# Two more products in two levels in group 4, and the last product in two levels from pieces loaded at the start of group 5

## The chip, the cores and the metric

The kernel runs on one core of one Trainium2 chip. A core has TensorE for matmuls, VectorE and ScalarE for elementwise work, GpSimd (POOL), and SyncE (SP); in this kernel the last two mostly issue DMAs, which sixteen DMA engines carry out. The metric is the device time of one execution in microseconds, as the median of several runs. Before the change it is 674.46 us (three runs, 673.37 to 674.55).

## What is computed

Linear attention with decay in blocks, and then an expert layer with the activation h - tanh(h):

```python
# q, k, v: (4, 8, 768, 64) float32; per head and block of 64 positions
intra = np.einsum('bhic,bhjc->bhij', qb, kb) * Dmask[None]
intra = np.einsum('bhij,bhjd->bhid', intra, vb)
inter = np.einsum('bhid,bhde->bhie', qb * lam_pow[None], kv_state)
out[:, :, sl] = intra + inter
kv_state = lam_block * kv_state + np.einsum('bhsd,bhse->bhde', kb_dec, vb)
...
x = attn_out.transpose(0, 2, 1, 3).reshape(3072, 512)
h = x @ w_in            # 512 x 2048
g = h - np.tanh(h)
return (g @ w_out)      # 2048 x 512
```

## The kernel before

**Groups.** The sequence of 768 is worked in six groups, g = 0 to 5, of 128 positions. With four batches a group holds 512 tokens. In each group the hidden layer has an "up" part (x times w_in, tanh) and a "down" part (times w_out). While group g is in its up and down parts, the attention of group g+1 is worked in pieces between them. Group 0 is computed plainly. In groups 1 to 5 the up and the down product are each done by a scheme of seven products instead of eight: the two factors are split into quarters, A11 to A22 and B11 to B22, sums S1 to S4 and T1 to T4 of quarters are formed, and P1 to P7 are multiplied: P1 = A11 B11, P2 = A12 B21, P3 = S4 B22, P4 = A22 T4, P5 = S1 T1, P6 = S2 T2, P7 = S3 T3.

**One level and two levels in the down part.** A product Pn of the down part is 256 tokens by 1024 hidden values by 256 outputs. `down` does it in one level: sixteen matmuls with 256 columns. `down_twice` uses the same scheme once more inside Pn: seven steps, 1 to 7, of four matmuls with 128 columns, in the order SUB = (1, 2, 6, 5, 7, 3, 4). For this it needs sums of quarters of the left factor (s1 to s4, by VectorE, 128 x 512 elements each) and of the right one. The latter are made once, in groups 1 to 4, by `factors_twice` (t1, t2, t3, t4), which writes them to the DRAM tensor `fine`; one-level factors lie in the DRAM tensor `factors`. `twice(g, n)` says which products are done in two levels. Before, P1 and P2 are so only in group 5, and P3 in every group but 1 and 5.

**Room for sums.** `sums_twice` (line 685) takes two tiles of a pool of four called "sums" and overwrites a quarter of the hidden layer for the third. P1 and P2 can't overwrite A11 and A12, which are used again; `sums_apart` (L699 to L702) takes four tiles for each, from the room of the q and k blocks, which is free in the last group. `factors_twice` (L593) takes three of the four "sums" tiles and makes t3 in the place of b12, a quarter that was loaded as a piece.

**Pieces.** The right factors come from DRAM in pieces of 256 KB by DMAs on GpSimd's queue, in a ring of seven places ("wb"). `pieces_of` gives the order of all pieces; `piece` issues loads up to seven ahead of their use. The quarters of the factor that `factors_twice` works on are pieces of this ring too. The fine factors of P1 are made in group 3, those of P2 in group 4, at fixed counts of the up products (`turns`).

**Banks.** A two-level product collects in two PSUM banks, y and zw. ScalarE copies y after steps 1, 6, 7 and 4 (L720), VectorE adds the parts of zw at the end (L727, L728). After P2, `first_out` adds P1 and P2 and stores a quarter of the output (L677), and `sums_once` (L636) forms S2 and later S4.

**Order in group 4 around the change.** In the up part, for each quarter u of the hidden layer, products 6, 5, 1 (of u+1), 7, 3 are worked; at u = 3 the down product P1 takes the place of product 1. Attention of group 5 comes in between: transposes of q and k by VectorE (L306), scores `sp` (L327), their mask (L331), outputs `op` (L375, L381). Then P2, P4, P5, P6, P7 and P3. Instructions are put in order by a list scheduler, for each engine, when the program is built[...].

**The end.** In group 5 `down_end` does P3 in one level, in three parts of 256, 128 and 128 columns; each is added to P5's result and stored on SP's queue while the next is multiplied.

The two conditions that the change edits:

```python
def twice(g, n):
    return n in TWICE and not (g == NG - 1 and n == 3) and not (g == 1 and n in (4, 7, 3)) and not (
        g < NG - 1 and n in (1, 2))
```

Of the kernel before, what the change touches and what calls it, by code (L numbers as in the profile page):

```python
# [16 lines left out]
BLK = 128  # L17
# [6 lines left out]
def kernel(  # L24
# [158 lines left out]
    SUB = (1, 2, 6, 5, 7, 3, 4)  # L183
    GI = 2
# [351 lines left out]
    def twice(g, n):  # L536
        return n in TWICE and not (g == NG - 1 and n == 3) and not (g == 1 and n in (4, 7, 3)) and not (
            g < NG - 1 and n in (1, 2))
# [8 lines left out]
    def pieces_of(g):  # L547
        if g >= GI:
            yield from ((g, ("in", 4), x) for x in (6, 5, 3))
        yield from ((g, ("quarter", t), x) for t in MADE_IN.get(g, ()) for x in range(4))  # L550
        for n in (1, 2, 4, 5, 6, 7):
            yield from ((g, n, x) for x in (SUB if twice(g, n) else range(NU)))
        if g == NG - 1:
            yield from ((g, 3, x) for x in range(NU))
            return
        for kind, x in in_turn(g):
            if kind == "down":
                yield g, 3, x
            elif x in (3, 5, 6):
                yield g + 1, ("in", 2), x  # L560
# [27 lines left out]
    def factors_twice(t):  # L588

        b11, b12, b21, b22 = (quarters.pop((t, i, j)) for i in range(2) for j in range(2))  # L590
        t1, t2, t4 = (late["pool"].tile([128, NU, 128], F32, name=f"wt{x}", tag="sums", bufs=4) for x in (1, 2, 4))
        for x, dst, a, b in ((5, t1, b12, b11), (6, t2, b22, t1), (7, b12, b22, b12), (4, t4, b21, t2)):
# [101 lines left out]
    def sums_apart(g, n):  # L694

        a11, a12, a21, a22 = quarter(g, n)
        s1, s2, s3, s4 = (late["blk"].tile([128, NP, BLK // 32, 32], F32, name="sblk", tag="blk").rearrange(
            "d p r a -> d p (r a)") for _ in range(4))
# [3 lines left out]
        nc.vector.tensor_tensor(s4, a12, s2, op=AL.subtract)  # L702
        low[g, n] = (s1, s2, s3, s4)

    def down_twice(g, n, zw):
        a11, a12, a21, a22 = quarter(g, n)
        apart = len(low[g, n]) == 4
        s1, s2, s3, s4 = low.pop((g, n)) if apart else (*low.pop((g, n)), a21, a12)
# [3 lines left out]
        for x, a, dst, keep in ((1, a11, y, o[:, 0:128]), (2, a12, zw[:, 0:128], None), (6, s2, y, o[:, 128:256]),  # L712
                                (5, s1, zw[:, 256:384], None), (7, s3, y, o[:, 384:512]), (3, s4, zw[:, 128:256], None),
                                (4, a22, y, o[:, 256:384])):
            wb = piece(g, n, x).rearrange("p m c -> p (m c)")
            for u in range(NU):
                nc.tensor.matmul(out=dst, lhsT=a[:, u, :], rhs=wb[:, ts(u, 128)], start=x in (1, 2) and u == 0,  # L717
                                 stop=u == NU - 1, skip_group_check=True)
            if keep is not None:
                nc.scalar.activation(keep, dst, AF.Copy)  # L720
            if x == 2 and not apart:
# [27 lines left out]

    def down_end(g):  # L750

        a, o = hidden(g, 21), res[g, 5].rearrange("q (m c) -> q m c", m=2)
        rows = out.rearrange("(b s) d -> s b d", b=B)[ts(g, BLK), 0:2, 256:512]
        wbs = [piece(g, 3, u) for u in range(NU)]
        for tag, m, c0, c1 in (("z", 0, 0, 256), ("w", 1, 0, 128), ("ya", 1, 128, 256)):
            t = bank("end", tag, 1)[:, 0:c1 - c0]
            for kt in range(KH):
                nc.tensor.matmul(out=t, lhsT=a[:, kt // 2, kt % 2, ts(m, 128)], rhs=wbs[kt // 2][:, kt % 2, c0:c1],
                                 start=kt == 0, stop=kt == KH - 1)
            nc.vector.tensor_tensor(o[:, m, c0:c1], o[:, m, c0:c1], t, op=AL.add)  # L760
            nc.sync.dma_start(out=rows[:, m, c0:c1], in_=o[:, m, c0:c1])
# [108 lines left out]
    for g in range(1, NG):  # L870
        last = g == NG - 1
        p0, p1 = attention(g + 1) if not last else ([], [])
# [93 lines left out]
```

## Time and profile before

| what | us | where it is read |
|---|---|---|
| median of three runs | 674.46 | times |
| profiled execution | 673.58 | times of the profiled run |
| its span, first to last instruction | 671.6 | page |
| TensorE, matmuls busy | 660.5 (98%) | page, part 1 |
| TensorE, weight loads busy | 576.3 (86%) | page, part 1 |
| VectorE busy | 491.2 (73%) | page, part 1 |
| ScalarE busy | 196.6 (29%) | page, part 1 |
| DMA, mean rate | 203 GB/s | page, part 2 |

The page shows one execution. Its span is shorter than the time measured, since some work lies before the first and after the last instruction. A matmul's recorded duration overlaps with the next one's, so the cost of a series is read from starts. "Idle before" in a timeline stands in brackets, with what ended it. The granted clock of TensorE is 1.000 over the whole run.

### The profile page before, as it was taken

How to read it: one execution, taken by the hardware profiler on the slowest of the kernel's cores; microseconds unless marked ns; L12 is line 12 of the kernel's file. 1: busy time of each engine (PE TensorE's matmuls, PEld its weight loads, DVE VectorE, ACT ScalarE, POOL GpSimd, SP SyncE). 2: the span in 40 equal slices, each digit the busy share in tenths (PEclk: the TensorE clock that was granted, in tenths of full speed). 3: DMA queues.
4: the chain of work that ended last, by engine and by line, in shares of the span. 5: the costliest groups of instructions: out<-in, count | busy, mean ns of one | idle time of the engine just before them, and what ended most of it. 6: DMA issues, size and time to landing. Idle time of an engine off the chain costs nothing.

```text
span 671.6 us, 13055 instructions
## 1 busy us (share of the span) xinstructions
PE 660.5 (98%) x4872; PEld 576.3 (86%) x4872; DVE 491.2 (73%) x892; ACT 196.6 (29%) x380; POOL 216.7 (32%) x373
## 2 busy tenths in 40 slices
PE   7899999999999999999999999999999999999998
PEld 6688855558888999987999988899988899988997
DVE  4798767993887772499896389988369978348963
ACT  4564433423331111333112242112333112334210
POOL 0001424217432424144345402254412244400451
PEclk9999999999999999999999999999999999999999
DMA  9979889869855977486998855597944686710695
GB/s 213 218 207 248 258 235 254 294 147 265 251 147 135 243 196 210 107 261 202 252 288 249 227 124 136 153 291 216 276 108 128 170 244 204 229 48 0 212 300 163
DMA packets 164958, 136.16 MB, mean 203 GB/s; under 512 B 134304, under 2 KB 135456, under 8 KB 164896
## 3 DMA queue, kind: packets, MB, share of 16 engines
q0 software_dynamic: 31216, 103.83, 48.8%
q1 hardware_dynamic: 133536, 31.50, 23.7%
q8 instruction: 39, 0.64, 0.4%
q14 instruction: 23, 0.19, 0.1%
q10 hardware_dynamic: 144, 0.00, 0.0%
HBM read 107.22 MB, written 28.05 MB: 201 GB/s over the span
## 4 chain that ended last, share of the span: by engine, by line
PE 81%; issue 9%; DMA 3%; POOL 3%; SPq 2%; DVE 1%; ACT 0%; POOLq 0%; DVEq 0%; ACTq 0%
PE y L433 11%; PE y L717 11%; PE op L795 8%; PE zw L717 8%; PE h L774 7%; PE z L433 7%; PE w L649 4%; PE y L649 4%; PE y L517 4%; PE plain L649 3%; PE sp L327 3%; PE op L381 3%; PE z L517 2%; POOL wb L614 2%; PE op L375 2%
## 5 line engine op out<-in xcount | busy, mean ns | idle before, releaser
L614 POOL DMA_DIRECT2D wb<-fine x161 | 86.7, 539 | 148.2 <-PE y L717 80.4
L441 ACT ACTIVATE th<-g 128x512 f32<-128x512 f32 x76 | 47.6, 630 | 94.8 <-DVE g L446 33.2
L433 PE MATMUL y<-xt,w 128*128 128x256 f32 x320 | 74.0, 380 | 0.0
L433 PEld LDWEIGHTS y<-xt,w 128*128 128x128 f32 x320 | 59.9, 190 | 9.0 <-ACT g L521 0.9
L720 ACT ACTIVATE q<-y 128x128 f32<-128x128 f32 x92 | 25.5, 277 | 133.8 <-PE y L717 132.9
L442 DVE TENSOR_TENSOR g<-g,th 128x512 f32<-128x512 f32 x76 | 51.8, 688 | 16.9 <-ACT th L441 16.8
L774 PE MATMUL h<-xt,w 128*128 128x256 f32 x256 | 56.5, 381 | 2.1 <-DVE w L271 2.1
L795 PE MATMUL op<-wt,g 128*128 128x512 f32 x128 | 56.5, 595 | 0.0
L774 PEld LDWEIGHTS h<-xt,w 128*128 128x128 f32 x256 | 48.2, 190 | 9.3 <-DVE w L271 1.5
L717 PE MATMUL y<-wb,g 128*128 128x128 f32 x416 | 55.4, 278 | 0.1
L717 PEld LDWEIGHTS y<-wb,g 128*128 128x128 f32 x416 | 50.5, 192 | 1.5 <-issue 0.6
L617 POOL DMA_DIRECT2D wb<-factors x48 | 25.9, 541 | 71.0 <-DVE wt L593 24.6
L795 PEld LDWEIGHTS op<-wt,g 128*128 128x128 f32 x128 | 23.8, 190 | 27.7 <-issue 26.5
L198 POOL DMA_DIRECT2D raw<-in_moe_w_out_dram x16 | 8.9, 553 | 91.0 <-DVE g L782 52.4
L433 PE MATMUL z<-tt,ws 128*128 128x256 f32 x160 | 38.1, 381 | 0.0
L433 PE MATMUL z<-xt,ws 128*128 128x256 f32 x160 | 37.9, 380 | 0.0
L433 PE MATMUL y<-tt,ws 128*128 128x256 f32 x160 | 37.8, 379 | 0.0
L717 PE MATMUL zw<-wb,g 128*128 128x128 f32 x272 | 35.9, 275 | 0.0
L331 DVE TENSOR_TENSOR ss<-sp,mask 128x512 f32<-128x512 f32 x48 | 31.0, 683 | 5.5 <-PE sp L327 5.5
L433 PEld LDWEIGHTS z<-xt,ws 128*128 128x128 f32 x160 | 30.2, 190 | 4.3 <-ACT g L449 0.2
L433 PEld LDWEIGHTS z<-tt,ws 128*128 128x128 f32 x160 | 29.6, 190 | 4.7 <-DVE g L469 0.8
L433 PEld LDWEIGHTS y<-tt,ws 128*128 128x128 f32 x160 | 30.1, 190 | 3.9
(181 smaller groups left out, 1325.6 us busy)
## 6 DMA issues: line engine op xcount, KB each, us to landing
wb<-fine POOLq DMA_DIRECT2D x161, 256.0 KB, 4.0
wb<-factors POOLq DMA_DIRECT2D x68, 256.0 KB, 4.6
raw<-in_moe_w_out_dram POOLq DMA_DIRECT2D x16, 512.0 KB, 5.1
v_nat<-in_v_dram SPq DMA_DIRECT2D x24, 256.0 KB, 5.3
factors<-wt POOLq DMA_DIRECT2D x8, 768.0 KB, 4.9
wb<-fine_in POOLq DMA_DIRECT2D x24, 256.0 KB, 4.2
fine<-wt POOLq DMA_DIRECT2D x21, 256.0 KB, 4.3
k_nat<-in_k_dram SPq DMA_DIRECT2D x20, 256.0 KB, 5.0
```

The source lines that it names most:

```text
L331: tied(g == 0, nc.vector.tensor_tensor(ss[:, j], sp[j], mask[:, j], op=AL.mult))
L433: nc.tensor.matmul(out=t[:, m, :], lhsT=wt[:, kt, ts(m, 128)], rhs=x[:, kt, :], start=first and m == 0 and kt == 0, stop=kt == 1, skip_gro ...
L441: nc.scalar.activation(th, src, AF.Tanh)
L442: nc.vector.tensor_tensor(dst(c), src, th, op=AL.subtract)
L517: nc.tensor.matmul(out=dst[:, ts(u, 128)], lhsT=a, rhs=b, start=x in (1, 2, 5) and u == 0, stop=True, skip_group_check=True)
L614: nc.gpsimd.dma_start(out=t.rearrange("p m c -> p (m c)"), in_=fine[TWICE.index(n_), SUB.index(x_)].rearrange("p u c -> p (u c)"))
L617: nc.gpsimd.dma_start(out=t, in_=factors[XAT[FACT[n_][1]]][:, 2 * x_:2 * x_ + 2, :])
L649: nc.tensor.matmul(out=t[:, m, :], lhsT=a[:, u, kt, ts(m, 128)], rhs=wb[:, kt, :], start=first and u == 0 and m == 0 and kt == 0, stop=u = ...
L717: nc.tensor.matmul(out=dst, lhsT=a[:, u, :], rhs=wb[:, ts(u, 128)], start=x in (1, 2) and u == 0, stop=u == NU - 1, skip_group_check=True)
L720: nc.scalar.activation(keep, dst, AF.Copy)
L774: tied(u == 0, nc.tensor.matmul(out=hm[c][:, m, :], lhsT=w1[u][:, i, a, ts(m, 128)], rhs=xt[0, t][:, i, :], start=m == 0 and i == 0, stop= ...
L795: nc.tensor.matmul(out=obank[b], lhsT=g, rhs=wt[:, 2 * a:2 * a + 2, :], start=kt == 0 and a == 0, stop=kt == KH - 1 and a == 1)
```

## The change

P1 and P2 are done in two levels in group 4 as well, and P3 in group 5. P1 and P2 work their steps in the order APART = (1, 5, 6, 2, 7, 3, 4). `sums_apart` makes three sums; the fourth is made inside the product after step 5, in the tile of s1. In group 4 the three tiles are those of k in natural layout, in group 5 blocks as before. `factors_twice` puts t3 in an own tile of the "sums" pool. `load_end`, called at the start of group 5, loads the seven fine pieces of P3 on SP's queue into the tiles of k and v; the four pieces of P3 leave GpSimd's stream. `down_end` does the seven steps from them, adds each quarter to P5's result as soon as it is complete, and stores it by itself.

```diff
--- before.py
+++ after.py
@@ -181,6 +181,8 @@
     factors = dram.tile([NX, 128, KH, 256], F32, name="factors")
 
     SUB = (1, 2, 6, 5, 7, 3, 4)
+
+    APART = (1, 5, 6, 2, 7, 3, 4)
     GI = 2
     TWICE = (3, 5, 6, 4, 7, 1, 2)
     fine = dram.tile([len(TWICE), len(SUB), 128, NU, 128], F32, name="fine")
@@ -534,8 +536,8 @@
     RING = 7
 
     def twice(g, n):
-        return n in TWICE and not (g == NG - 1 and n == 3) and not (g == 1 and n in (4, 7, 3)) and not (
-            g < NG - 1 and n in (1, 2))
+        return n in TWICE and not (g == 1 and n in (4, 7, 3)) and not (
+            g < NG - 2 and n in (1, 2))
 
     def in_turn(g):
 
@@ -549,9 +551,8 @@
             yield from ((g, ("in", 4), x) for x in (6, 5, 3))
         yield from ((g, ("quarter", t), x) for t in MADE_IN.get(g, ()) for x in range(4))
         for n in (1, 2, 4, 5, 6, 7):
-            yield from ((g, n, x) for x in (SUB if twice(g, n) else range(NU)))
+            yield from ((g, n, x) for x in (range(NU) if not twice(g, n) else APART if n < 3 else SUB))
         if g == NG - 1:
-            yield from ((g, 3, x) for x in range(NU))
             return
         for kind, x in in_turn(g):
             if kind == "down":
@@ -588,8 +589,9 @@
     def factors_twice(t):
 
         b11, b12, b21, b22 = (quarters.pop((t, i, j)) for i in range(2) for j in range(2))
-        t1, t2, t4 = (late["pool"].tile([128, NU, 128], F32, name=f"wt{x}", tag="sums", bufs=4) for x in (1, 2, 4))
-        for x, dst, a, b in ((5, t1, b12, b11), (6, t2, b22, t1), (7, b12, b22, b12), (4, t4, b21, t2)):
+        t1, t2, t3, t4 = (late["pool"].tile([128, NU, 128], F32, name=f"wt{x}", tag="sums", bufs=4)
+                          for x in (1, 2, 3, 4))
+        for x, dst, a, b in ((5, t1, b12, b11), (6, t2, b22, t1), (7, t3, b22, b12), (4, t4, b21, t2)):
             tc.keep_in_program_order(nc.vector.tensor_tensor(dst, a, b, op=AL.subtract))
             nc.gpsimd.dma_start(out=fine[TWICE.index(MADE[t]), SUB.index(x)], in_=dst)
             if MADE[t] in (1, 2) and x in (5, 6, 4):
@@ -693,31 +695,41 @@
 
     def sums_apart(g, n):
 
+
         a11, a12, a21, a22 = quarter(g, n)
-        s1, s2, s3, s4 = (late["blk"].tile([128, NP, BLK // 32, 32], F32, name="sblk", tag="blk").rearrange(
-            "d p r a -> d p (r a)") for _ in range(4))
+        if g == NG - 1:
+            sums = [late["blk"].tile([128, NP, BLK // 32, 32], F32, name="sblk", tag="blk").rearrange(
+                "d p r a -> d p (r a)") for _ in range(3)]
+        else:
+            sums = [io.tile([128, H, D], F32, name="sk", tag="k", bufs=3).rearrange("p (u v) d -> p u (v d)", u=NU)
+                    for _ in range(3)]
+        s1, s2, s3 = sums
         nc.vector.tensor_tensor(s1, a21, a22, op=AL.add)
         nc.vector.tensor_tensor(s2, s1, a11, op=AL.subtract)
         nc.vector.tensor_tensor(s3, a11, a21, op=AL.subtract)
-        nc.vector.tensor_tensor(s4, a12, s2, op=AL.subtract)
-        low[g, n] = (s1, s2, s3, s4)
+        low[g, n] = (s1, s2, s3)
 
     def down_twice(g, n, zw):
         a11, a12, a21, a22 = quarter(g, n)
-        apart = len(low[g, n]) == 4
-        s1, s2, s3, s4 = low.pop((g, n)) if apart else (*low.pop((g, n)), a21, a12)
+        apart = n < 3
+        s1, s2, s3, s4 = (*low[g, n], low[g, n][0]) if apart else (*low.pop((g, n)), a21, a12)
         y = bank("y2", "ya" if n in (4, 6, 3, 1) else "yb", 1)[:, 0:128]
         zw = bank("zw", zw, 1)
         o = res[g, n] = otile(f"q{n}")
-        for x, a, dst, keep in ((1, a11, y, o[:, 0:128]), (2, a12, zw[:, 0:128], None), (6, s2, y, o[:, 128:256]),
-                                (5, s1, zw[:, 256:384], None), (7, s3, y, o[:, 384:512]), (3, s4, zw[:, 128:256], None),
-                                (4, a22, y, o[:, 256:384])):
+        steps = {1: (a11, y, o[:, 0:128]), 2: (a12, zw[:, 0:128], None), 6: (s2, y, o[:, 128:256]),
+                 5: (s1, zw[:, 256:384], None), 7: (s3, y, o[:, 384:512]), 3: (s4, zw[:, 128:256], None),
+                 4: (a22, y, o[:, 256:384])}
+        order = APART if apart else SUB
+        for x in order:
+            a, dst, keep = steps[x]
             wb = piece(g, n, x).rearrange("p m c -> p (m c)")
             for u in range(NU):
-                nc.tensor.matmul(out=dst, lhsT=a[:, u, :], rhs=wb[:, ts(u, 128)], start=x in (1, 2) and u == 0,
-                                 stop=u == NU - 1, skip_group_check=True)
+                nc.tensor.matmul(out=dst, lhsT=a[:, u, :], rhs=wb[:, ts(u, 128)],
+                                 start=x in (1, 5 if apart else 2) and u == 0, stop=u == NU - 1, skip_group_check=True)
             if keep is not None:
                 nc.scalar.activation(keep, dst, AF.Copy)
+            if x == 5 and apart:
+                nc.vector.tensor_tensor(s4, a12, s2, op=AL.subtract)
             if x == 2 and not apart:
                 nc.vector.tensor_tensor(a12, a12, s2, op=AL.subtract)
             if x != STEPS[-1]:
@@ -747,18 +759,55 @@
         for _ in steps:
             pass
 
+    ends = {}
+
+    def load_end():
+
+        for x, tag, bufs in zip(SUB, "kkkvvvv", (3, 3, 3, 4, 4, 4, 4)):
+            t = ends[x] = io.tile([128, H, D], F32, name="wend", tag=tag, bufs=bufs).rearrange("p h d -> p (h d)")
+            nc.sync.dma_start(out=t, in_=fine[TWICE.index(3), SUB.index(x)].rearrange("p u c -> p (u c)"))
+
     def down_end(g):
 
-        a, o = hidden(g, 21), res[g, 5].rearrange("q (m c) -> q m c", m=2)
+        a11, a12, a21, a22 = quarter(g, 3)
+        s1, s2 = low.pop((g, 3))
+        y, zw = bank("y2", "ya", 1)[:, 0:128], bank("zw", "z", 1)
+        o, f = otile("q3"), res[g, 5]
         rows = out.rearrange("(b s) d -> s b d", b=B)[ts(g, BLK), 0:2, 256:512]
-        wbs = [piece(g, 3, u) for u in range(NU)]
-        for tag, m, c0, c1 in (("z", 0, 0, 256), ("w", 1, 0, 128), ("ya", 1, 128, 256)):
-            t = bank("end", tag, 1)[:, 0:c1 - c0]
-            for kt in range(KH):
-                nc.tensor.matmul(out=t, lhsT=a[:, kt // 2, kt % 2, ts(m, 128)], rhs=wbs[kt // 2][:, kt % 2, c0:c1],
-                                 start=kt == 0, stop=kt == KH - 1)
-            nc.vector.tensor_tensor(o[:, m, c0:c1], o[:, m, c0:c1], t, op=AL.add)
-            nc.sync.dma_start(out=rows[:, m, c0:c1], in_=o[:, m, c0:c1])
+
+        def add(c, src):
+            nc.vector.tensor_tensor(f[:, ts(c, 128)], f[:, ts(c, 128)], src, op=AL.add)
+
+        def leave(c):
+            nc.sync.dma_start(out=rows[:, c // 2, ts(c % 2, 128)], in_=f[:, ts(c, 128)])
+
+        for x, a, dst, keep in ((1, a11, y, 0), (2, a12, zw[:, 0:128], None), (6, s2, y, 1),
+                                (5, s1, zw[:, 256:384], None), (7, a21, y, 3), (3, a12, zw[:, 128:256], None),
+                                (4, a22, y, None)):
+            for u in range(NU):
+                nc.tensor.matmul(out=dst, lhsT=a[:, u, :], rhs=ends[x][:, ts(u, 128)], start=x in (1, 2) and u == 0,
+                                 stop=u == NU - 1, skip_group_check=True)
+            if keep is not None:
+                nc.scalar.activation(o[:, ts(keep, 128)], dst, AF.Copy)
+            if x == 2:
+                nc.vector.tensor_tensor(a12, a12, s2, op=AL.subtract)
+            elif x == 6:
+                add(0, o[:, 0:128])
+                add(0, zw[:, 0:128])
+                leave(0)
+            elif x == 5:
+                add(1, o[:, 128:256])
+                f5 = f.rearrange("q (i c) -> q i c", i=2)[:, :, 128:256]
+                nc.vector.tensor_tensor(f5, f5, zw[:, 256:384][:, None, :].to_broadcast([128, 2, 128]), op=AL.add)
+            elif x == 7:
+                add(3, o[:, 384:512])
+                leave(3)
+            elif x == 3:
+                add(1, dst)
+                leave(1)
+            elif x == 4:
+                add(2, dst)
+                leave(2)
 
 
     def up_plain(u, cs):
@@ -869,6 +918,8 @@
     up(1, 0, 1)
     for g in range(1, NG):
         last = g == NG - 1
+        if last:
+            load_end()
         p0, p1 = attention(g + 1) if not last else ([], [])
         for u in range(NU):
             if u + 1 == NU and twice(g, 1):
```

## The prediction

> **What bounds the kernel now.** I read the page's shares and chain first, then TensorE's timeline over the last two groups, then the timelines of the engines that feed it. Two lines of the page:
>
> ```profile
> PE 660.5 (98%) x4872; PEld 576.3 (86%) x4872; DVE 491.2 (73%) x892; ACT 196.6 (29%) x380; POOL 216.7 (32%) x373
> ...
> PE 81%; issue 9%; DMA 3%; POOL 3%; SPq 2%; DVE 1%; ACT 0%; POOLq 0%; DVEq 0%; ACTq 0%
> ```
>
> Matmuls hold 81% of the chain that ended last, and weight loads alone fill 86% of the span. The list of waits gives TensorE 7.7 us in the whole trace, all but 0.7 of it on tiles of the first stage (h, sp, idle, tp, kv). So TensorE's queue is the clock: what is taken out of it shortens the run, provided that nothing it needs comes late. TensorE's timeline, groups 4 and 5 (start, duration, engine, line, operation, tiles, shapes, count; a float32 matmul is two instructions, hence x32 for sixteen):
>
> ```profile
> 517.88 7.07 PE L649 MATMUL y<-wb,g 128*128 128x256 f32 x32
> 524.78 1.89 PE L433 MATMUL z<-xt,ws 128*128 128x256 f32 x8
> 526.60 2.06 PE L327 MATMUL sp<-qt,kt 64*128 64x128 f32 x32
> 528.59 7.17 PE L649 MATMUL w<-wb,g 128*128 128x256 f32 x32
> 535.69 1.10 PE L375 MATMUL op<-qd,state 64*64 64x128 f32 x32
> ...
> 554.47 1.06 PE L717 MATMUL zw<-wb,g 128*128 128x128 f32 x8
> 555.36 1.06 PE L717 MATMUL y<-wb,s 128*128 128x128 f32 x8
> ...
> 661.30 7.19 PE L758 MATMUL end<-wb,g 128*128 128x256 f32 x48
> ```
>
> Starts, not durations, give the cost: durations overlap. One-level P1 of group 4 takes 524.78 - 517.88 = 6.90, P2 535.69 - 528.59 = 7.10; a step of a two-level product takes 555.36 - 554.47 = 0.89, seven of them 6.25. Now VectorE in group 4:
>
> ```profile
> 512.93 0.69 DVE L442 TENSOR_TENSOR g<-g,th 128x512 f32<-128x512 f32 x1 [0.16 <-ACT th L441]
> ...
> 517.03 0.69 DVE L593 TENSOR_TENSOR wt<-wb,wt 128x512 f32<-128x512 f32 x1
> 517.63 0.70 DVE L306 STREAM_TRANSPOSE qt<-q_blk 128x512 f32<-128x512 f32 x1
> ...
> 521.21 0.68 DVE L451 TENSOR_TENSOR g<-g,y 128x512 f32<-128x512 f32 x1
> 521.81 0.68 DVE L452 TENSOR_TENSOR g<-g,y 128x512 f32<-128x512 f32 x1
> 522.41 0.68 DVE L636 TENSOR_TENSOR g<-gS,g 128x512 f32<-128x512 f32 x1
> 523.01 1.28 DVE L442 TENSOR_TENSOR g<-g,th 128x512 f32<-128x512 f32 x2
> ```
>
> Bracketed idle time is nearly absent: VectorE is 96% busy from 517.6 to 538.6 (20.09 of 21.0 us by the stretches' busy times), one operation per 0.60 us. This is the only place where the change meets a second full engine. Last, GpSimd's issues of pieces there:
>
> ```profile
> 486.75 1.73 POOL L617 DMA_DIRECT2D wb<-factors  x3
> 500.80 0.54 POOL L617 DMA_DIRECT2D wb<-factors  x1 [12.32 <-DVE wt L593]
> ...
> 509.74 0.54 POOL L617 DMA_DIRECT2D wb<-factors  x1 [2.11 <-DVE wb L593]
> 510.28 0.54 POOL L594 DMA_DIRECT2D fine<-wb  x1
> 514.39 0.54 POOL L617 DMA_DIRECT2D wb<-factors  x1 [3.58 <-DMA fine<-wb]
> 518.01 0.54 POOL L594 DMA_DIRECT2D fine<-wt  x1 [3.08 <-DVE wt L593]
> 518.55 0.54 POOL L617 DMA_DIRECT2D wb<-factors  x1
> ```
>
> The ring's seven places are shared with the four quarters from which P2's fine factors are made, so pieces come one by one as quarters are released.
>
> [...] so a wait put in VectorE's queue holds everything behind it, as at 175.02, where L593 waited 0.31 us for a store and L464 stood behind. [...] after SP's 256 KB store at 637.95 the landing of pieces rose from 2.9 to 5.2 us.
>
> **Part by part: TensorE.** P1: 6.90 to 6.25, -0.65. P2: 7.10 to 6.25 plus 0.10 for the switch of operand seen at such starts, -0.75. Last P3: 668.50 - 661.30 = 7.20 to 6.35, -0.85. Sum -2.25 us. The tail stays: a 128x128 add (0.29) and a 64 KB store (668.84 to 670.37) end both. The six other adds of the last product are 0.29 to 0.42 each and its a12 0.69; P7's four (2.2 us together) and these, 4.8 in all, fit in its 6.25 us, and its SP queue has six stores of 0.35 us. ScalarE's ten more copies of 0.28 us (3 for P1, 4 for P2, 3 for P3) hide under 29% load.
>
> **VectorE in group 4.** Added for each of P1 and P2: three sums and the fourth, 4 x 0.60, and two adds of the zw bank, about 0.38 each: 3.15, so 6.3 us together, where there is next to no idle time. What can give way is work that is due later: eight L636 (for P6 and P3) and P5's three sums, 6.6 us, all before 538.6. So it just fits, if the order is good. In group 5 the three sums of P1 stand between L452 and L469 at 615.80 to 619; the like place here is 512.7 to 516. They push the transposes by 1.8 - 0.3 = 1.5 us, to end at 522.7. Then L451, L452, s4 (ready after P1's step 5, which ends at 519.7) at 523.9 to 524.5, and the two L442, which complete A12, at 525.7. P1's step 3 wants s4 at 517.88 + 5 x 0.89 = 522.3; product 3 of up (1.73) and sp (1.99) are there to fill this. P2's first sum can run from 525.7 and its step 5 wants it at 517.88 + 6.25 + 1.73 + 1.99 + 0.89 = 528.7: 3.0 us for P4's two sums and P2's own. I take 0 for this, since group 5 ran P4's and P2's first sums right behind L442 (624.83 and 625.43); its bounds are 0 and 4.4 (below).
>
> **Pieces of P1.** Seven instead of four: three at 486.75, the fourth at 500.80, the fifth and sixth at about 509.7, since b12 is free after t3 and no longer at the landing of its store (514.39). The seventh waits for b21, read by t4 at 517.03, which the sums may push by 1.5: issue between 518.0 and 520.0, landing after 4.7 to 5.4 us (518.55 landed at 524.01), so 523 to 525.4 against a need at 523.25, or 525 with product 3 before it. Taken: +0.2; bounds 0 and 2.1. P2's pieces are issued from 519 on, at P1's steps, and are due from 528: covered.
>
> **t3's own tile.** It takes the fourth of four places called sums. In group 1 t3 would start at 174.02 but its place is freed by t1's store, which landed at 175.00; t4's by a store that landed at 177.41. If L464 stays behind t4, it goes from 175.63 to 178.0, and product 3, which adds to the bank that it reads, from 176.78 to 178.7: 1.9 us. If L464 goes ahead, nothing. The second set repeats this with 0.25. In group 2 twelve tiles instead of nine go through the four places (about 1.2 us at 295), but quarters come free earlier and may save its two TensorE waits, 0.54 and 0.15. Taken: +0.2 in all; bounds -0.7 and +3.3.
>
> **DMAs.** load_end puts 7 x 256 KB on SP's queue, idle from 529 to 638, where they start as soon as places come free: three at P2's end, two after att_out at 538, two at 563; all before the stretch 588 to 617 with 26 GB/s. In 538.6 to 551.5 the engines are 81% busy at 240 GB/s; when saturated they move about 300, so 1.3 MB more are some 4 us of their time. A piece has about 5.2 us from issue to use and lands in 2.9 to 4.7 there. Taken 0; bounds 0 and 1.5. The last four loads of GpSimd's queue (656.04 to 658.72) go away, worth up to the two waits of 0.1 us near them.
>
> **Sum.** -2.25 + 0.2 + 0.2 = -1.85. The profiled execution took 673.58 (span 671.6 and 2.0 around it), so 671.7 for one like it; it lies 0.9 below the median of the runs shown, 674.46, which is my basis: 672.6.
>
> **Rivals.** First, VectorE gives the two products' gain back. If product 3 and sp are moved ahead of P1's step 3, their followers (L469, L442, L472, L473, four L331: 4.8 us), P1's zw adds (0.75) and P4's two sums (1.2) come before P2's sum: 525.7 + 6.75 + 0.6 = 533.1. With op (2.95) moved into the hole, TensorE has work until 531.7 and waits 1.4. Then 674.46 - 1.85 + 1.4 = 674.0. For it: 96% busy; against: P4's and P2's sums may fill the waits for tanh. A burst of DMAs in P5 (1.5) gives 674.1 and goes with this case.
> Second, slower, by the same late sum, where op stays behind P2 in TensorE's fixed order: the wait is 533.1 - 528.7 = 4.4, and 674.46 - 2.25 + 4.4 = 676.6. It decides from 3.6 us of wait on (2.25 and the 1.35 of the bound), that is, if P2's first sum ends after 532.3. For it: eleven operations have an older claim on the queue; against: this trace shows TensorE's order often rearranged around what is late. That the products are not two-level at all can't be: the pieces' addresses and the order of steps follow from twice alone.
>
> **How the numbers follow.** Forecast 0.40, first rival 0.27, second 0.33 (its chance takes in sums of small waits that I priced near nothing). About 0.2%, 1.35 us, is what a measurement of this kernel can tell from no change: below 673.1 is faster, above 675.8 slower. The forecast's own range is 671.4 to 673.1: the low end has 0.9 of vanished small waits and no stall. For 8 in 10 both rivals are taken in, up to 677.0.
>
> **What would show it.** Right: L649 gone from group 4, L717 x56 for each of its P1 and P2, no idle of TensorE at its steps 5 and 3, the last product 6.3 us long, the wend loads landed before 570. Wrong: an idle of TensorE before P2's second step with VectorE as releaser (rivals), before P1's last step with a DMA, in group 1 before L433 z with L464, or P5's pieces landing later than 5.2 us after issue.

## The result and the profile after

The changed kernel takes 680.95 us (median of four runs, 679.48 to 682.84); the kernel before took 674.38 (four runs, 673.37 to 674.55). The ratio on record is 1.0115 with a 95% interval of 1.0095 to 1.0135, slower by 1.1%; the two medians given here stand 1.0% apart. The prediction, 672.6 with a range up to 677.0, was wrong in sign, and the range did not hold the result. The profiled execution took 680.28 us, with a span of 678.2 (671.6 before).

From the page of the changed kernel, the busy times and the chain that ended last:

```profile
PE 661.7 (98%) x4928; PEld 577.4 (85%) x4928; DVE 501.0 (74%) x912; ACT 198.4 (29%) x390; POOL 218.5 (32%) x375
...
PE 74%; issue 10%; DMA 6%; DVE 4%; POOL 3%; SPq 2%; ACT 1%; POOLq 0%; DVEq 0%; ACTq 0%
```

The shares of busy time look as before; the chain doesn't. Matmuls hold 74% of it where they held 81%, and DMA and VectorE rose from 3% to 6% and from 1% to 4%. TensorE still has all the work, but now it waits. Its list of waits names where (engine, tile, line, releaser: total us, times, longest):

```profile
PE y L651 <- issue: 1.6, 1, 1.6
PE y L727 <- DMA wb<-fine: 1.6, 1, 1.6
...
PE zw L727 <- DMA wb<-fine: 1.1, 3, 0.5
...
PE op L377 <- DVE ss L333: 0.7, 1, 0.7
PE zw L727 <- DVE sk L707: 0.4, 1, 0.4
PE zw L788 <- DVE q L779: 0.3, 1, 0.3
```

Of these six the kernel before had only the first, with 0.5 us, and 0.2 us more there for a piece. The three waits of the third line lie in group 3 (0.54), in P4 of group 4 (0.41) and in group 5 (0.19). The shift between equal matmuls of the two traces gives the place of the whole 6.6 us:

| stretch | forecast, us | measured, us | from matmul starts (before, after) |
|---|---|---|---|
| up to P1 of group 2 | +0.2 | +1.16 | 311.02, 312.18 |
| from there to the end of group 3 | 0 | +1.39 | 473.09, 475.64 |
| up part, P1 and P2 of group 4, to P4's first | -1.2 | +3.04 | 538.62, 544.21 |
| P4 and P5 of group 4, to the scores `sp` | 0 | +1.12 | 551.81, 558.52 |
| from there to the last product | 0 | -0.12 | 661.30, 667.89 |
| last product, and the tail | -0.85 | 0.0 (-0.17, +0.18) | 668.49, 674.91 (its end); 671.6, 678.2 (ends of the spans) |

Each trace is one execution: in the two traces of one and the same kernel, end_fix and end_fix_again below, the same stretch differs by up to 0.8 us. So the first two rows need the runs that follow; 3.04 is well beyond this.

TensorE's timeline of the changed kernel over P1 and P2 of group 4 (start, duration, engine, line, operation, tiles, shapes, count, idle before):

```profile
524.21 1.06 PE L727 MATMUL y<-wb,sk 128*128 128x128 f32 x8
525.11 0.60 PE L435 MATMUL z<-xt,ws 128*128 128x256 f32 x2
527.32 1.13 PE L727 MATMUL y<-wb,g 128*128 128x128 f32 x8 [1.61 <-DMA wb<-fine]
528.28 1.03 PE L435 MATMUL z<-xt,ws 128*128 128x256 f32 x4
...
533.64 0.43 PE L377 MATMUL op<-qd,state 64*64 64x128 f32 x2
534.75 1.10 PE L377 MATMUL op<-qd,state 64*64 64x128 f32 x30 [0.69 <-DVE ss L333]
535.78 1.52 PE L383 MATMUL op<-ss,v_nat 128*64 128x128 f32 x22
537.75 1.16 PE L727 MATMUL zw<-wb,sk 128*128 128x128 f32 x8 [0.45 <-DVE sk L707]
...
549.50 1.13 PE L727 MATMUL zw<-wb,g 128*128 128x128 f32 x8 [0.41 <-DMA wb<-fine]
```

The last line is P4. Besides three waits in P1 and P2, 2.75 us together, one sees products cut up: up's product 3 (`z<-xt,ws`) runs in parts between P1's steps, and `op` stands inside P2. VectorE's timeline of the same kernel shows both places where it is late, group 2 and group 4:

```profile
303.20 0.69 DVE L595 TENSOR_TENSOR wt<-wb,wt 128x512 f32<-128x512 f32 x1 [0.91 <-DVE g L453]
...
304.41 0.68 DVE L454 TENSOR_TENSOR g<-g,y 128x512 f32<-128x512 f32 x1
...
518.22 0.69 DVE L709 TENSOR_TENSOR sk<-g 128x512 f32<-128x512 f32 x1
...
520.88 0.68 DVE L595 TENSOR_TENSOR wt<-wb,wt 128x512 f32<-128x512 f32 x1
...
530.24 0.42 DVE L739 TENSOR_TENSOR q<-q,zw 128x256 f32<-128x256 f32 x1 [1.50 <-PE zw L727]
...
537.01 0.68 DVE L707 TENSOR_TENSOR sk<-g 128x512 f32<-128x512 f32 x1
```

In group 2, L595 waits 0.91 us and L454, which reads the bank that TensorE wants next, stands behind it; before, the same operation had no wait (301.73). The releaser named, L453, had long been done; a store of an earlier tile (L596), issued at 297.88, landed at 303.12, just ahead. In group 4, P1's sums push t4 (L595) to 520.88; VectorE then idles 1.50 us at 530.24, because P1 is late; and P2's first sum comes only at 537.01. GpSimd's queue shows what t4 holds up:

```profile
512.26 1.08 POOL L616 DMA_DIRECT2D wb<-fine  x2 [2.11 <-DVE wt L595]
...
521.86 0.55 POOL L596 DMA_DIRECT2D fine<-wt  x1 [7.98 <-DVE wt L595]
522.40 2.82 POOL L616 DMA_DIRECT2D wb<-fine  x5
```

P1's seventh piece is issued at 522.40, behind the store of t4, lands at 527.18, and its first consumer starts at 527.32.

### The profile page after: what moved, and what is told of

Its sections match the earlier page's. It is cut to its first block, busy times and chain, and to the rows that moved or that the text cites. A ratio compares the mean times of both kernels' runs of the same rounds, so it can differ in the third digit from the quotient of the medians.

```text
span 678.2 us, 13232 instructions
## 1 busy us (share of the span) xinstructions
PE 661.7 (98%) x4928; PEld 577.4 (85%) x4928; DVE 501.0 (74%) x912; ACT 198.4 (29%) x390; POOL 218.5 (32%) x375
## 4 chain that ended last, share of the span: by engine, by line
PE 74%; issue 10%; DMA 6%; DVE 4%; POOL 3%; SPq 2%; ACT 1%; POOLq 0%; DVEq 0%; ACTq 0%
PE y L435 10%; PE y L727 10%; PE op L844 8%; PE h L823 7%; PE zw L727 7%; PE z L435 6%; PE y L519 3%; DMA wb<-fine 3%; PE w L651 3%; PE plain L651 3%; PE y L651 3%; PE sp L329 3%; PE op L383 2%; POOL wb L616 2%; PE z L519 2%
## 5 line engine op out<-in xcount | busy, mean ns | idle before, releaser
L616 POOL DMA_DIRECT2D wb<-fine x175 | 94.5, 541 | 171.8 <-PE y L727 87.7
L730 ACT ACTIVATE q<-y 128x128 f32<-128x128 f32 x100 | 27.7, 277 | 149.9 <-PE y L727 149.1
L727 PE MATMUL y<-wb,g 128*128 128x128 f32 x448 | 60.1, 278 | 1.6 <-DMA wb<-fine 1.6
L727 PEld LDWEIGHTS y<-wb,g 128*128 128x128 f32 x448 | 54.6, 192 | 3.8 <-ACT th L443 2.0
L727 PE MATMUL zw<-wb,g 128*128 128x128 f32 x288 | 38.3, 275 | 0.4 <-DMA wb<-fine 0.4
L727 PEld LDWEIGHTS zw<-wb,g 128*128 128x128 f32 x288 | 35.1, 192 | 0.6 <-issue 0.6
L333 DVE TENSOR_TENSOR ss<-sp,mask 128x512 f32<-128x512 f32 x48 | 31.0, 683 | 5.2 <-PE sp L329 5.2
```

The lines of the kernel that those rows point to most:

```text
L333: tied(g == 0, nc.vector.tensor_tensor(ss[:, j], sp[j], mask[:, j], op=AL.mult))
L616: nc.gpsimd.dma_start(out=t.rearrange("p m c -> p (m c)"), in_=fine[TWICE.index(n_), SUB.index(x_)].rearrange("p u c -> p (u c)"))
```

## The experiments

All ratios are to the kernel before, run on the same chip at the same time, with 95% intervals. 0.1% is 0.67 us.

**One part alone.** t3_alone is the kernel before with only t3's own tile.

```diff
-        for x, dst, a, b in (..., (7, b12, b22, b12), (4, t4, b21, t2)):
+        for x, dst, a, b in (..., (7, t3, b22, b12), (4, t4, b21, t2)):
```

> The kernel before with t3 in an own tile of the four sums tiles, and nothing else. Theory 1 (t3's tile lets VectorE wait for a store in group 2): TensorE waits some 1.6 us before the first matmul of P1 in group 2 instead of 0.5, all else as before, time +1.1 us, ratio 1.0017. Theory 2 (the whole loss of 6.6 us lies in group 4, the 2.5 us before it are chance of one execution): no change, ratio 1.000.

Measured: 1.0021 (1.0011 to 1.0030), 1.4 us. Its trace has a wait of 1.2 us at P1 of group 2 and 0.6 us for pieces at P5 of group 3, and nothing in group 1. So the tile does cost, by the mechanism described for group 1, but in group 2, where VectorE meets a place whose store has not landed.

sums5 is the changed kernel with five places of the sums pool instead of four.

```diff
-... tag="sums", bufs=4)
+... tag="sums", bufs=5)
```

> The changed kernel with five tiles in the sums pool instead of four. Theory 1: the wait in group 2 goes, TensorE is 1.1 us earlier from there on and stays so to the end: 1.1 us below the changed kernel, near 679.8, ratio to before 1.008. Theory 2: as the changed kernel, 1.0097.

Measured: 1.0069 (1.0050 to 1.0088), against 1.0115: more than the 1.1 us of theory 1. Group 2's shift is gone (-0.08), and most of group 3's with it (+0.49 instead of +1.39). Whether group 3's came from group 2's delay or from the same pool is not separated. The fifth place takes away most of the wait and not all: t3 still waits for a store there, 0.27 us here and 0.30 to 0.58 in late_loads, best, own_s4 and own_s4_sp. Group 4's waits stay: 1.8 for a piece, 0.7 and 0.4 for VectorE.

end_alone is the kernel before with only the last P3 in two levels; p12_alone has only P1 and P2 of group 4 in two levels, with t3 in the place of b12. Both have the change's code for the steps and sums of P1 and P2, which is used in group 5 too, and end_alone has its `load_end` and `down_end`; the excerpt shows the conditions only.

```diff
 end_alone:
-    ... not (g == NG - 1 and n == 3) and ...
 p12_alone:
-            g < NG - 1 and n in (1, 2))
+            g < NG - 2 and n in (1, 2))
```

> The kernel before with the last product in two levels from early loaded pieces, and nothing else (t3 in b12's place, P1 and P2 of group 4 in one level). Theory A (the end by itself gains, the early loads cost nothing where P1 and P2 don't crowd the DMAs): -0.35 to -0.85 us, ratio 0.9990. Rival B (the seven loads run into the pieces of P4 and P5 in group 4 and hold TensorE there): +0.3 to +1.0 us, with waits of TensorE for wb<-fine in group 4.

> The kernel before with P1 and P2 in two levels in group 4 (steps and sums as in the change), t3 in b12's place and the end in one level. Theory A (the loss sits in group 4's P1 and P2: P1's last piece waits for b21, VectorE then waits for P1's end, and P2's sums come late): +3 us or more, ratio 1.0045 to 1.008, with TensorE's wait before P1's last step of 1.6 us or more. Rival B (it is the early loads and t3's tile that make the loss): -1.4 us, ratio 0.998.

Measured: end_alone 0.9999 (0.9988 to 1.0010); the last product takes 7.02 us as in the changed kernel (7.19 before). p12_alone 1.0053 (1.0034 to 1.0072), 3.6 us lost where 1.4 were to be won, with the three waits of group 4 (1.7, 0.7, 0.4). p1_only is sums5 with P2 in one level:

```diff
-            g < NG - 2 and n in (1, 2))
+            g < NG - 2 + (n == 2) and n in (1, 2))
```

> The changed kernel with five sums tiles, but P2 of group 4 in one level. Ring theory: the wait before P1's last step stays (1.8 us), P2 needs no sums; the loss of P1 by itself is about 1.8 - 0.65 + 0.5 of switching; ratio 1.002 to 1.003. Capacity theory: with half of the added VectorE work most of the loss goes, ratio 1.000 to 1.001.

Measured: 1.0010 (1.0001 to 1.0018), as the capacity theory had it and below the ring theory's range; the wait for P1's piece is 1.0. So of sums5's loss P2 makes the larger part.

**The piece behind t4.** early_t4 is sums5 with P2's factors made in steps of two counts instead of three, so that t4 comes 9.7 us earlier (509.11 instead of 518.83; the expectation had put it at some 5).

```diff
-NG - 2: (7 * NU + 10 * NU - 4, ((6, 4),), 3)}
+NG - 2: (7 * NU + 10 * NU - 4, ((6, 4),), 2)}
```

> The changed kernel with five sums tiles and with the factor of P2 made at every second step of group 4's up part instead of every third, so that t4, the last reader of b21, stands some 5 us earlier in VectorE's queue. Ring theory (P1's seventh piece gets b21's place too late; TensorE waits 1.8 us for it and VectorE 1.5 us for P1's end, which makes P2's sums late): the wait for wb<-fine before P1's last step goes, P2's first sum comes in time, -2.5 to -3.5 us against the kernel with five sums tiles, ratio to before 1.002 to 1.003. Capacity theory (VectorE has too much to do in group 4, the piece is late beside it): the wait for the piece goes, but TensorE waits for sk or ss as long instead; -0.5 us or less, ratio 1.006.

Measured: 1.0028 (1.0015 to 1.0040), 2.7 us better than sums5, as the ring theory had it. The wait for the piece is gone. TensorE's timeline of early_t4 shows what comes next:

```profile
531.21 1.08 PE L377 MATMUL op<-qd,state 64*64 64x128 f32 x26
533.60 1.13 PE L727 MATMUL y<-wb,sk 128*128 128x128 f32 x8 [1.30 <-issue]
534.65 0.44 PE L377 MATMUL op<-qd,state 64*64 64x128 f32 x6
```

"issue" names no releaser, but VectorE wrote P2's second sum at 532.81 to 533.49, just ahead, after four masks of the scores (L333).

**The order of the sums.** sums2_first is early_t4 with P2's sums written ahead of these masks; VectorE's order follows.

```diff
+            if not last and u + 1 == NU and twice(g, 2):
+                sums_apart(g, 2)
             if not last and u > 1:
                 run(p0[u - 2:u - 1])
```

> As early_t4 (five sums places, P1's t4 two counts earlier), and P2's three sums of group 4 are written ahead of the masks of the scores, so that VectorE does them first. Theory (order on VectorE): the 1.3 us wait of TensorE at P2 in early_t4 came because P2's first sum stood behind the masks that follow the scores; with it ahead the wait is under 0.4 us and the ratio falls from early_t4's 1.0028 to 1.000 to 1.001. Rival (VectorE simply has too much to do): the masks and with them op are late by as much, the same 1.2 to 1.6 us stand at op instead of P2, and the ratio stays at 1.0025 to 1.003.

Measured: 1.0035 (1.0024 to 1.0046), no gain. The wait of 1.30 went, as the theory had it, and from P1's first to P4's first matmul 22.12 us became 21.32 (20.74 before the change). But 0.6 us for P2's fourth sum and 0.4 us for one of P5 came in its place.

**Loads and GpSimd.** late_loads is sums5 with `load_end`'s seven loads on GpSimd's queue after the first pieces of group 5; pool_sums is sums5 with the three sums of P1 and of P2 in group 4 on GpSimd.

```diff
 late_loads:
-            nc.sync.dma_start(out=t, in_=fine[...])
+            tc.keep_in_program_order(nc.gpsimd.dma_start(out=t, in_=fine[...]))
 pool_sums:
-        nc.vector.tensor_tensor(s1, a21, a22, op=AL.add)
+        eng.tensor_tensor(s1, a21, a22, op=AL.add)
```

> As sums5, but the seven loads for the last P3 are on GpSimd's queue behind the first pieces of group 5 (about 588), not on SP's queue from 537 on. Theory (the loads collide with the pieces of P4 in group 4): TensorE's two or three waits on wb from 545 to 552, 0.7 to 1.0 us together, go, and the ratio falls from sums5's 1.0069 to 1.0055 to 1.006. Rival (P4's pieces are late because P1 and P2 take fourteen pieces where eight were): the waits stay, 1.0066 to 1.0072.

> The changed kernel with five sums tiles, with the three sums of P1 and of P2 in group 4 made by GpSimd instead of VectorE. Capacity theory: VectorE has 3.6 us less to do, t4 is no longer pushed back and P2's sums don't queue: -2 us or more against the kernel with five sums tiles, ratio 1.004 or less. Ring theory: t4 comes 1.8 us earlier, so the wait before P1's last step shrinks or goes too, unless GpSimd's issue of the pieces stands behind its own sums; then the wait stays or grows, ratio 1.006 or more.

Measured: late_loads 1.0071 (1.0054 to 1.0088). The interval holds both forecasts, so the time does not decide; the traces do. The time to landing of the five pieces issued between 540 and 545 us, and P4's sixth step, first in sums5 and then in late_loads:

```profile
DMA to landing us min/median/max: 4.9/5.6/6.4
547.36 1.13 PE L727 MATMUL zw<-wb,g 128*128 128x128 f32 x8 [0.32 <-DMA wb<-fine]
```

```profile
DMA to landing us min/median/max: 3.0/3.8/4.1
546.76 1.06 PE L727 MATMUL zw<-wb,g 128*128 128x128 f32 x8
```

With the loads moved the waits in P4 are gone, and P4 takes what it took before the change; sums5 lost 0.76 us there by matmul starts. So the loads do collide with P4's pieces. The ratio does not show it: from P5 to the last product late_loads is 0.5 us slower than sums5 in these two traces. It waits 0.64 us for a piece at 647.39 (sums5 0.16); whether that comes from the moved loads is not shown.

pool_sums 1.0083 (1.0063 to 1.0102), with 4.3 us of waits for the fourth sum, the longer one 2.76. GpSimd takes 1.28 to 1.73 us for a sum that takes VectorE 0.69, and issues no piece meanwhile.

**The last product.** In the changed kernel its step 5 writes the bank zw while an add that reads another part of zw has still to be done. All engines of the changed kernel at this place:

```profile
670.74 0.28 DVE L779 TENSOR_TENSOR q<-q,zw 128x128 f32<-128x128 f32 x1
...
671.07 1.16 PE L788 MATMUL zw<-wend,s 128*128 128x128 f32 x8 [0.34 <-DVE q L779]
```

end_fix is end_alone with this add, and its store, moved behind step 5; end_fix_again is the same kernel once more; end_fix_late has the late loads too.

```diff
             elif x == 6:
                 add(0, o[:, 0:128])
-                add(0, zw[:, 0:128])
-                leave(0)
             elif x == 5:
+                add(0, zw[:, 0:128])
+                leave(0)
                 add(1, o[:, 128:256])
```

> The kernel before with the last product in two levels alone, and the add that reads step 2 from bank zw moved from behind step 6 to behind step 5. Theory (TensorE's step 5 writes the bank that VectorE's add still has to read, and waits 0.34 us and restarts): the wait goes and TensorE's last product takes 6.25 to 6.35 us instead of 6.85; -0.5 us against the end alone, ratio to before 0.9990 to 0.9993. Rival (the wait is hidden by something later, such as the stores at the end): no change, 0.9999.

> The same kernel as end_fix. If the last product's saving of about 1.1 us is real, 0.998 to 0.999; if 0.9984 was a favourable draw, 0.9993 to 1.0003.

> As end_fix (only the last P3 in two levels, the add of bank zw moved behind step 5), with its seven loads on GpSimd's queue at the start of group 5. There are no waits on pieces in group 4 in end_fix, so both theories expect its ratio again, 0.998 to 0.999; if the loads cost something hidden there, 0.9975 or less; if on GpSimd's queue they hold up the pieces of group 5, 1.000 or more.

Measured: end_fix 0.9984 (0.9971 to 0.9997), again 0.9991 (0.9979 to 1.0003), with late loads 0.9998 (0.9988 to 1.0008). The wait is gone and the last product takes 6.51 us instead of 7.02 (6.25 to 6.35 was expected). 0.7 us is 0.1%, below what these runs tell from no change; the intervals allow it and don't prove it.

**All repairs.** best takes early_t4, sums2_first, the moved add and the late loads together.

> All repairs together: five sums places, t4 earlier, P2's sums ahead of the masks, loads late, the add of bank zw behind step 5. If each of the measured losses is a separate cause, what is left is the saving of products: P1 and P2 together -0.5 to -1.4 us, the last product -1.1, ratio 0.9965 to 0.9985, faster than end_fix's 0.9984 or like it. If VectorE's load in group 4 is the limit whatever the order, P1 and P2 still cost +1 us or more and the ratio is 0.9995 to 1.001.

Measured: 1.0028 (1.0019 to 1.0037). The separate losses don't add up to separate gains. Its matmuls show why. I took each matmul's start-to-start time, and the median of its kind in the same trace as its usual cost. From P1's first to P4's first matmul, before: 19.31 us of usual cost and 1.43 of excess. best: 18.03 and 3.29. So the matmuls did get cheaper by 1.28, nearly the forecast 1.40; 1.86 of waits and switches ate it. Most of them lie where a product is split around its fourth sum, which can be made only after step 5, as it is put in the tile of s1. own_s4 gives it a tile of its own; own_s4_sp is the same with the loads on SP's queue.

```diff
+            sums.append(late["pool"].tile([128, NU, 128], F32, name="s4", tag="sums", bufs=5))
...
+        nc.vector.tensor_tensor(s4, a12, s2, op=AL.subtract)
...
-            if x == 5 and apart:
-                nc.vector.tensor_tensor(s4, a12, s2, op=AL.subtract)
```

> As best, but the fourth sum of P1 and P2 has a tile of its own (in group 4 a place of the sums pool, in group 5 a fourth block) and is made with the other three, not after step 5. Theory (the tie of s4 to step 5 splits the products): P1's and P2's seven steps run without a hole, the waits of 0.33 and 0.61 us and 0.7 us or more of switches go, from P1's first to P4's first matmul 21.3 us becomes 19.5 to 20.2 (20.74 in the kernel before), ratio 1.0005 to 1.0015. Rival (VectorE has too much to do): the hole moves elsewhere (masks, gS, P4's sums), the stretch stays at 21 us or more, ratio 1.0025 or more.

> As own_s4, with the seven loads of the last P3 on SP's queue as in the changed kernel. late_loads showed no gain from moving them, so both theories expect own_s4's ratio within 0.0010; more than that means that GpSimd's queue pays for the late loads.

Measured: own_s4 1.0013 (1.0004 to 1.0021), own_s4_sp 1.0007 (0.9997 to 1.0018); neither is faster than the kernel before. Both theories are right, one after the other. TensorE's timeline of own_s4:

```profile
518.97 1.05 PE L729 MATMUL y<-wb,g 128*128 128x128 f32 x8
...
538.62 1.16 PE L729 MATMUL y<-wb,g 128*128 128x128 f32 x8
...
544.13 1.16 PE L729 MATMUL zw<-wb,g 128*128 128x128 f32 x8 [0.78 <-DVE g L734]
...
552.17 1.16 PE L729 MATMUL zw<-wb,gS 128*128 128x128 f32 x8 [1.10 <-DVE gS L734]
```

From P1's first to P4's first (538.62) it is 19.65 us, 1.09 less than before: the gain is there. Then P4 and P5 wait 1.88 us for their own fourth sums (L734), and by matmul starts they take 2.35 us more than before. The busy times by stretch of own_s4_sp, all engines (after the length: PE, PEld, DVE, ACT, POOL, clock, DMA share, GB/s):

```profile
518.00:528.00 10.00, 10.00 (x85) 9.12 (x85) 9.90 (x18) 2.37 (x6) 3.77 (x7) 1.00 0.66 183
528.00:538.00 10.00, 10.00 (x136) 9.59 (x136) 10.00 (x19) 1.74 (x5) 3.76 (x7) 1.00 0.88 280
538.00:548.00 10.00, 9.22 (x86) 8.86 (x83) 9.90 (x18) 2.47 (x7) 5.04 (x9) 1.00 0.94 311
548.00:558.00 10.00, 8.89 (x90) 8.34 (x90) 9.60 (x18) 1.11 (x4) 3.76 (x7) 1.00 0.65 203
```

and of the kernel before:

```profile
518.00:528.00 10.00, 10.00 (x65) 8.69 (x65) 9.39 (x16) 2.37 (x4) 3.24 (x6) 1.00 0.72 181
528.00:538.00 10.00, 10.00 (x100) 8.60 (x100) 9.85 (x17) 0.12 (x1) 2.15 (x4) 1.00 0.59 149
538.00:548.00 10.00, 10.00 (x97) 9.83 (x94) 6.74 (x12) 2.57 (x8) 5.58 (x10) 1.00 0.75 227
548.00:558.00 10.00, 10.00 (x103) 9.71 (x103) 8.78 (x16) 1.29 (x5) 4.69 (x9) 1.00 0.74 227
```

Before, VectorE had 5.2 us of idle time in these 40 us (34.8 busy), 4.5 of it after 538. The change adds 6.3 us of work to them. own_s4_sp has 39.4 busy: the debt used up the idle time of P4 and P5, and what is left over is TensorE's wait. How much of it is lack of time and how much is order stays open. VectorE's timeline of own_s4_sp at P4's fourth sum:

```profile
541.96 1.29 DVE L638 TENSOR_TENSOR g<-g,g 128x512 f32<-128x512 f32 x2
543.17 0.69 DVE L734 TENSOR_TENSOR g<-g,s 128x512 f32<-128x512 f32 x1
543.77 0.69 DVE L638 TENSOR_TENSOR g<-g,g 128x512 f32<-128x512 f32 x1
```

L638 here makes S4, which is due for P3, the last product of the group; L734 is what TensorE waits for. No run has these two in another order.

**Taking sums off VectorE.** pool_s2 and pool_s4 are own_s4_sp with four sums of group 4 on GpSimd, those of S2 (due for P6) or of S4 (due for P3).

```diff
-            nc.vector.tensor_tensor(...)
+            (nc.gpsimd if g == NG - 2 and dst == 11 else nc.vector).tensor_tensor(...)
```

> As own_s4_sp, with the four sums of group 4 that form S2 (due only for P6, from about 559) done by GpSimd instead of VectorE, where they took 2.4 us between 534 and 543. Theory (VectorE is short of time): TensorE's waits of 0.78 and 1.11 us at P4 and P5 shrink to under 0.5 us together, ratio from 1.0007 to 0.998 to 0.9995. Rival (GpSimd's sums, 1.3 to 1.7 us each in pool_sums, hold up the issue of pieces on its queue): new waits on wb of 0.5 us or more in P2 or P4, ratio 1.0005 to 1.003.

> As own_s4_sp, with the four sums of group 4 that form S4 (due for P3) done by GpSimd; on VectorE they stood right ahead of the two sums that were late. Theory (VectorE is short of time): the waits at P4 and P5 shrink to under 0.5 us together, ratio 0.998 to 0.9995. Rival (GpSimd's pieces are held up, since P4's are issued back to back there): new waits on wb in P4 of 0.5 us or more, ratio 1.0005 to 1.003.

Measured: 1.0054 (1.0036 to 1.0072) and 1.0090 (1.0065 to 1.0114). This is slower than both theories allow, and only a small part is the rival's mechanism: pool_s2 waits 0.46 us for a piece, pool_s4 none in group 4. The long waits, 1.89 and 4.23 us, are for P4's fourth sum, and VectorE itself was held. The timelines of pool_s2, of VectorE and of GpSimd:

```profile
525.30 4.69 DVE L444 TENSOR_TENSOR g<-g,th 128x512 f32<-128x512 f32 x1
```

```profile
525.12 1.28 POOL L638 TENSOR_TENSOR g<-gS,g 128x512 f32<-128x512 f32 x1
526.34 0.57 POOL L616 DMA_DIRECT2D wb<-fine  x1
526.93 2.49 POOL L638 TENSOR_TENSOR g<-gS,g 128x512 f32<-128x512 f32 x2
```

An operation of 0.69 us lasts 4.69 while GpSimd does three sums beside it. So these two runs took work off VectorE and its time too, and they don't settle whether a VectorE with 2.4 us less to do would bring the gain. pool_s4 also waited 2.6 us at P1 of group 2, where own_s4_sp waited 1.2. VectorE's timeline has the same wait for a store as t3_alone, 1.74 us where own_s4_sp has 0.57:

```profile
304.39 0.69 DVE L595 TENSOR_TENSOR wt<-wb 128x512 f32<-128x512 f32 x1 [1.74 <-DMA fine<-wt]
```

The store it waits for took 5.74 us to land and those before it 7.3 to 7.5, against 4.7 to 5.6 in own_s4_sp; why they were slow in this execution is not known.

## Why the prediction was wrong

**TensorE, -2.25: near in size.** The matmuls of P1 and P2 cost 1.28 us less (forecast 1.40), the last product 0.68 in end_fix (forecast 0.85).

**VectorE in group 4, 0: the step that failed.** "What can give way is work that is due later ... So it just fits, if the order is good." In the changed kernel it did not fit. The stretch up to P4's first matmul came 3.04 us later, where -1.2 was forecast. Of these 4.24 us the late piece of P1 is 1.61; the rest, some 2.6, is the waits of 0.69 and 0.45 for VectorE and the cutting of products around its late sums. With the order repaired, in own_s4, the work did give way; but the prediction closed its count at 538.6 and did not ask what the delayed work meets behind it. There P4 and P5 have late sums of their own, and VectorE's idle time was what kept them in time. At its best, in own_s4, the term is 1.9 us of waits. The bound of 4.4 held it.

**A tie that was read and not priced.** "s4 (ready after P1's step 5)" was treated as a time to be met by other work. The scheduler met it by cutting products around it. own_s4 against best: 1.67 us of TensorE (21.32 to 19.65).

**Pieces of P1, +0.2: the mechanism right, the size wrong.** The issue was foreseen "between 518.0 and 520.0"; it came at 522.40, which less the shift of 2.55 is 519.9, and landed 4.8 us later, inside the forecast 523 to 525.4. The need was put at 525, "with product 3 before it"; only two of product 3's eight matmul instructions stood there, so the need was about 523 and the wait 1.61. It also idled VectorE for 1.50, which made P2's sums later still. early_t4 took back 2.7 us in all. The bound was 2.1.

**t3's own tile, +0.2: the mechanism right, the place and size wrong.** 1.4 us alone. In the changed kernel it is 1.16 up to P1 of group 2 and a part of group 3's 1.39; sums5 takes most of both away. Group 1, for which the mechanism was worked out, shows no shift; group 2, where it was expected to be balanced by quarters that come free earlier, shows it all.

**DMAs, 0: wrong in size, inside its bound of 1.5.** P4 of group 4 took 0.99 us longer in the changed kernel and 0.76 in sums5, but no longer than before in late_loads and p12_alone, which have no loads there, and in end_alone and p1_only, which have the loads and P2 in one level. In early_t4, where P2's sums come earlier beside the same loads, it took 0.13 longer. So it takes both: P4's pieces issued late, behind P2's late sums, and the loads beside them. A sign of being wrong, pieces "landing later than 5.2 us after issue", was named for P5's, of which the latest took 5.4, and came true for P4's: up to 6.7 us here. What the prediction read at 637.95 as the effect of one store was only in part that: the landing had risen from 2.9 to about 4 us before the store was issued. The prediction's "about 300" GB/s for full engines, the most that the page of the kernel before shows in a slice, was no limit: the changed kernel moved 344 GB/s from 548 to 558 us, with the engines 96% busy.

**Last product, -0.85.** The switch of one bank between writer and reader was missing: "fit in its 6.25 us" counted VectorE's time and not the order in which it frees zw. It cost 0.51 us, so that in the changed kernel the last product gained only 0.17.

**The rivals.** The second had the mechanism and its condition: P2's first sum ended at 537.69, less the shift of 2.55 at 535.1, against the 532.3 from which it decides. Its price of 4.4 us of wait did not come as one wait, since `op` was moved into the hole in part. The loss is beyond it because the piece, the tile and the loads came on top. Each of these was given its likely value near nothing, and all came out at their upper sides together; the piece and the loads hang on VectorE's lateness too, so they were bound to come together, and the range up to 677.0 left no room for their sum.

## What to carry to other kernels

Where an edit saves time on the full engine by giving work to another, count the second engine's idle time not over the stretch of the edit but up to where the debt can be repaid (here P4 and P5, which waited 1.88 us in own_s4), and list the deadlines in between. A result that is made in the middle of a series, because it reuses a tile of that series, cuts the series in two: price the cut (1.67 us of TensorE here, own_s4 against best), or pay for the tile. A late reader holds up a ring of loads (here t4; early_t4 took back 2.7 us): find who reads last before each added piece.

## What was not expected of the hardware

In pool_s2 and pool_s4 GpSimd's sums held back operations of VectorE. In pool_s2 an operation of 0.69 us took 4.69 and ended 0.57 us after the third sum beside it; in pool_s4 four operations of VectorE, of 0.68 or 0.69 us by themselves, took 1.43 to 1.75 and ended 0.54 to 0.56 us after the sum beside them. The masks of the scores were not held: in pool_s2 three of them took 1.88 us beside the sum at 535.82, as in pool_s4 with none beside them. What the two engines contend for was not shown.

In pool_s4 TensorE waited 4.23 us until 548.70, and then ran at half speed. Its busy times by stretch (columns as above, the clock after POOL):

```profile
548.00:550.00 2.00, 1.30 (x6) 1.30 (x7) 1.90 (x4) 0.00 (x0) 0.12 (x1) 0.50 0.84 289
550.00:552.00 2.00, 2.00 (x11) 2.00 (x11) 1.82 (x5) 0.00 (x0) 0.54 (x1) 0.50 0.52 207
552.00:554.00 2.00, 2.00 (x13) 2.00 (x12) 2.00 (x4) 0.28 (x1) 0.54 (x1) 0.57 0.53 131
```

The granted clock is 0.50 for 4 us, and the shift to the kernel before grows from 1.12 us ahead of the wait to 5.51 at the first matmul behind it and 8.00 at 553.87, where matmuls are at their usual pace again: a wait of 4.2 us cost 6.9. In pool_sums the clock fell around a wait of 2.76 us (0.72 in the mean of 536 to 542, and the step behind the wait lasted 2.07 us where 1.16 is usual); the 1.89 of pool_s2 left it at 1.00. Whether the length of the wait alone decides was not shown.

In best a switch between series cost TensorE time by itself: by the excess over usual start-to-start times, about 0.09 us into an operation of another shape and 0.25 to 0.35 on the way back (sp or op to a product).
